# Decode attention over a long cache: heads loaded in pairs with 64 KB rows into three shared buffers, in a hand-scheduled program with a hardware loop

## The chip, the cores and the metric

The kernel runs on one core of a Trainium2 chip. The metric is the device time of one execution in microseconds (us). A "span" is the length of the profiled execution; a run's time is 1.7 to 2.0 us longer than its span (except in run 11). Engines: PE multiplies matrices (PEld is its weight load), DVE does elementwise work and reductions, ACT evaluates functions, SP issues the loads, and 16 DMA engines move the data.

## The reference, cut to what matters

```python
q = (x @ wq).reshape(B, Sq, H, Dh)             # B = Sq = 1, H = 32, Dh = 128
scores = einsum('bhqd,bhkd->bhqk', q, k_cache) * Dh ** -0.5     # Sk = 16384
p = softmax(scores)
a = einsum('bhqk,bhkd->bhqd', p, v_cache).reshape(...) @ wo     # 512 outputs
b = gated MLP of x                             # 512 -> 1792 -> 512, "gMLP" below
out = g * a + (1 - g) * b                      # g: one sigmoid gate
```

K and V are bf16, 4 MiB per head each: 256 MiB for 32 heads, read once. With one query there are about two operations for each loaded element, so the loads are the work.

## The kernel before

Each head's K is one load of 4 MiB with a contiguous 32 KB row in each of 128 partitions, three K buffers deep; V likewise, two deep. The scores are a multiplication on DVE by the broadcast q, then a sum over d by matmuls with an identity and a DVE reduce. The value product has two forms:

```python
def load_k(h):
    t = kv.tile([P, NJ * Dh], BF16, name="k_t", tag="k", bufs=3)      # 32 KB rows
    nc.sync.dma_start(out=t[:], in_=k_src[h])

def scores_mult(h):
    for ks in halves(h):                                              # DVE, in place
        nc.vector.tensor_tensor(out=ks, in0=ks, in1=qh, op=ALU.mult)

def attend(h):              # narrow: V stationary, p moving (1 column); the last 3 heads
    for j in range(NJ):
        nc.tensor.matmul(o_ps[:, h:h + 1], lhsT=v3[:, j, :], rhs=p_sb[h][:, j:j + 1], ...)

def attend_wide(h):         # wide: p stationary, V moving (512 columns); the other 29
    for t in range(NG):
        nc.tensor.matmul(d_ps[32 * g:32 * g + R, :], lhsT=p_sb[h][:, t * R:(t + 1) * R],
                         rhs=vtile[h][:, t * R * Dh:(t + 1) * R * Dh], ...)
# the wide form is followed, every four heads, by a drain (ACT copies d_ps out)
# and a collect (PE picks from the copy each head's own rows)
...                         # gMLP in the middle, about head 22; wo last:
for a, b in ((0, 16), (16, 24), (24, 30), (30, 32)):
    nc.sync.dma_start(out=wo_t[:, a * D:b * D], in_=wo_src[:, a * D:b * D])
```

The softmax here doesn't subtract the row's maximum and nothing guards it: scores larger than these inputs give would overflow.

## Time and profile before

| | before |
|---|---|
| time, median of 12 runs | 661.48 us (661.35 to 662.01) |
| DMA engines busy | 98.8% of the span, for 279.58 MB |
| PE, DVE busy | 77%, 50% |
| instruction fetches by DMA, 16 KB each | 21 |
| packets of 32 KB | 8,192, median 1216 ns |

The page of the kernel before: busy times (engine, us, share, instructions), then the DMA queues (packets, MB, share of 16 engines' span).

```profile
PE 508.3 (77%) x2661; PEld 216.6 (33%) x2661; DVE 331.4 (50%) x167; ACT 28.2 (4%) x88; POOL 0.7 (0%) x6
...
DMA packets 10583, 279.96 MB, mean 424 GB/s; under 512 B 1213, under 2 KB 1214, under 8 KB 1598
...
q1 hardware_dynamic: 10556, 279.58, 98.8%
q8 instruction: 21, 0.34, 0.2%
```

The windows view of the kernel before. The last three columns are the granted PE clock, the DMA share and GB/s.

```profile
core 0: us, PE busy (x) PEld busy (x) DVE busy (x) ACT busy (x) POOL busy (x), PEclk, DMA share, GB/s
...
200.00:300.00 100.00, 80.00 (x337) 32.62 (x337) 53.41 (x21) 3.38 (x14) 0.00 (x0) 0.91 1.00 431
300.00:400.00 100.00, 78.32 (x329) 31.36 (x329) 51.92 (x22) 2.49 (x11) 0.00 (x0) 0.91 1.00 431
...
630.00:640.00 10.00, 7.65 (x144) 5.07 (x142) 1.29 (x3) 0.40 (x2) 0.00 (x0) 0.84 0.95 399
```

Read the pair "1.00 431" first: every DMA engine is busy all the time, while PE and DVE have a fifth and half of the time free. Nothing that only frees PE or DVE can help in this stretch.

The end of the kernel before, in the chain of waits in order of time (start us, us, what):

```profile
632.06 23.85 DMA wo_t<-in_A_wo_dram
655.90 0.05 issue
655.95 1.03 PE a_ps L363 x32
...
657.53 0.21 DVE resT L370
```

The span ends when the loads end, plus about 4 us: 655.90 to 659.8.

### The profile page before, as it was taken

The numbers are of one execution on the slowest core, as the hardware profiler recorded it, in microseconds if no ns is written. First come the engines' busy times: TensorE is split into PE (matmuls) and PEld (weight loads), VectorE is DVE, ScalarE is ACT, GpSimd is POOL, SyncE is SP. The second block draws the span as 40 slices with busy tenths as digits, with TensorE's granted clock in tenths as the row PEclk, the third lists the DMA queues.
The fourth block names the chain that finished last, engine by engine and source line by source line (L and its number), as shares of the span: only waits on it lengthen the run. The fifth ranks groups of instructions, "written<-read, shape, count | busy, mean of one in ns | idle before, by whom it ended". The sixth has DMA issues, their size and how long they took to land.

```text
span 659.8 us, 5835 instructions
## 1 busy us (share of the span) xinstructions
PE 508.3 (77%) x2661; PEld 216.6 (33%) x2661; DVE 331.4 (50%) x167; ACT 28.2 (4%) x88; POOL 0.7 (0%) x6
## 2 busy tenths in 40 slices
PE   2666987786987777898777987739879788877774
PEld 0222432332333323333222333314325233333353
DVE  2567565554456554445654445624566554455600
ACT  0200000000000000000000000000000210000000
POOL 0000000000000000000000000000000000000000
PEclk9888998899988989979878998878979899988975
DMA  9999999999999999999999999999999999999996
GB/s 381 433 425 440 420 439 429 428 433 426 439 421 435 435 426 433 428 431 430 431 434 428 429 433 427 432 430 433 428 431 430 434 427 432 429 430 433 427 415 246
DMA packets 10583, 279.96 MB, mean 424 GB/s; under 512 B 1213, under 2 KB 1214, under 8 KB 1598
## 3 DMA queue, kind: packets, MB, share of 16 engines
q1 hardware_dynamic: 10556, 279.58, 98.8%
q8 instruction: 21, 0.34, 0.2%
q14 instruction: 4, 0.03, 0.0%
q10 hardware_dynamic: 2, 0.00, 0.0%
HBM read 279.58 MB, written 0.00 MB: 424 GB/s over the span
## 4 chain that ended last, share of the span: by engine, by line
DMA 66%; PE 22%; DVE 10%; SPq 1%; issue 0%; DVEq 0%
DMA k_t<-in_A_k_cache_dram 53%; PE s_ps L248 11%; DVE k_t L242 10%; PE d_ps L277 10%; DMA w_in<-in_B_w_in_dram 5%; DMA v_t<-in_A_v_cache_dram 4%; DMA wo_t<-in_A_wo_dram 4%; SPq L78 1%; PE o_ps L265 1%; PE o_ps L288 0%; PE a_ps L363 0%; SPq L339 0%; DVE s_sb L255 0%; SPq L62 0%; PE rT_ps L368 0%
## 5 line engine op out<-in xcount | busy, mean ns | idle before, releaser
L248 PE MATMUL s_ps<-k_t,ident 128*128 128x512 bf16 x1024 | 270.3, 428 | 124.6 <-DVE k_t L242 124.6
L242 DVE TENSOR_TENSOR k_t<-k_t,qb 128x8192 bf16<-128x8192 bf16 x64 | 280.3, 4422 | 165.2 <-DMA k_t<-in_A_k_cache_dram 165.2
L277 PE MATMUL d_ps<-v_t,p_t 128*4 128x512 bf16 x928 | 205.0, 379 | 0.0
L248 PEld LDWEIGHTS <-ident 128*128 128x128 bf16 x1024 | 110.2, 108 | 280.8 <-issue 182.1
L277 PEld LDWEIGHTS <-p_t 128*4 128x4 bf16 x928 | 76.4, 85 | 126.2 <-issue 12.3
L255 DVE TENSOR_REDUCE s_sb<-s_ps 128x64 f32<-128x512 f32 x64 | 44.2, 690 | 126.1 <-PE s_ps L248 126.1
L258 ACT ACTIVATE p_t<-s_sb 128x128 bf16<-128x128 f32 x32 | 9.9, 310 | 396.2 <-DVE s_sb L255 396.2
L106 PE MATMUL q_ps<-wq_t,xb 128*128 128x512 bf16 x32 | 9.2, 458 | 10.5 <-DMA wq_t<-in_A_wq_dram 10.5
L265 PE MATMUL o_ps<-p_t,v_t 128*128 128x1 bf16 x384 | 10.7, 164 | 5.7 <-DMA v_t<-in_A_v_cache_dram 5.7
L265 PEld LDWEIGHTS <-v_t 128*128 128x128 bf16 x384 | 10.3, 100 | 6.1 <-DMA v_t<-in_A_v_cache_dram 6.1
L283 ACT COPY d_sb<-d_ps 128x512 f32<-128x512 f32 x8 | 4.7, 586 | 169.8 <-PE d_ps L277 169.8
L106 PEld LDWEIGHTS <-xb 128*128 128x128 bf16 x32 | 3.6, 113 | 15.8 <-issue 12.4
L288 PEld LDWEIGHTS o_ps<-pick,d_sb 128*128 128x128 f32 x64 | 8.4, 192 | 1.1
L288 PE MATMUL o_ps<-pick,d_sb 128*128 128x4 f32 (+1 forms) x64 | 7.6, 242 | 0.0
L363 PE MATMUL a_ps<-o,wo_t 128*128 128x1 bf16 x128 | 3.9, 166 | 4.3 <-DMA wo_t<-in_A_wo_dram 4.3
L109 DVE CAST qb<-q_ps 128x512 bf16<-128x512 f32 x1 | 0.7, 691 | 11.3 <-PE q_ps L106 11.3
L258 ACT ACTIVATION_READ_ACCUMULATOR p_t<-s_sb 128x1 f32 x32 | 6.0, 188 | 0.0
L350 DVE TENSOR_TENSOR o_sb<-o_ps,rl 128x32 bf16<-128x32 f32 x1 | 0.2, 192 | 11.5 <-PE o_ps L265 11.5
L363 PEld LDWEIGHTS <-wo_t 128*128 128x128 bf16 x128 | 3.7, 104 | 4.5 <-DMA wo_t<-in_A_wo_dram 4.5
L111 ACT CAST qb<-q_ps 128x512 bf16<-128x512 f32 x7 | 4.1, 586 | 16.3 <-PE q_ps L106 16.3
L366 DVE CAST res<-a_ps 128x4 bf16<-128x4 f32 x1 | 0.2, 163 | 8.0 <-PE a_ps L363 8.0
L179 PE MATMUL z_ps<-xb,w_in 128*128 128x1 bf16 x56 | 3.1, 192 | 0.0
(65 smaller groups left out, 25.1 us busy)
## 6 DMA issues: line engine op xcount, KB each, us to landing
k_t<-in_A_k_cache_dram SPq DMA_DIRECT2D x32, 4096.0 KB, 36.7
v_t<-in_A_v_cache_dram SPq DMA_DIRECT2D x31, 4096.0 KB, 27.9
wq_t<-in_A_wq_dram SPq DMA_DIRECT2D x1, 4096.0 KB, 12.4
v_t<-in_A_v_cache_dram SPq DMA_DIRECT2D x1, 2048.0 KB
v_t<-in_A_v_cache_dram SPq DMA_DIRECT2D x2, 1024.0 KB, 16.8
wo_t<-in_A_wo_dram SPq DMA_DIRECT2D x1, 2048.0 KB, 20.4
w_in<-in_B_w_in_dram SPq DMA_DIRECT2D x1, 1792.0 KB, 33.1
wo_t<-in_A_wo_dram SPq DMA_DIRECT2D x1, 1024.0 KB, 22.4
```

The costliest lines, as they stand in the source:

```text
L78: nc.sync.dma_start(out=t[:, a * Dh:b * Dh], in_=v_src[h][:, a * Dh:b * Dh])
L106: nc.tensor.matmul(q_ps[:, :], lhsT=xb[:, c, :], rhs=wq[:, c, nb * QB:(nb + 1) * QB], start=(c == 0), stop=(c == DC - 1))
L111: nc.scalar.copy(out=qb[:, nb * QB:(nb + 1) * QB], in_=q_ps[:, :])
L242: nc.vector.tensor_tensor(out=ks, in0=ks, in1=qh, op=ALU.mult)
L248: nc.tensor.matmul(s_ps[:, :, :], lhsT=ident[:, :], rhs=ks[:, :, i * W:(i + 1) * W], start=(i == 0), stop=(i == NS - 1))
L255: nc.vector.tensor_reduce(out=s_sb[:, s * NH:(s + 1) * NH], in_=s_part[h, s][:, :, :], axis=AX.X, op=ALU.add)
L258: nc.scalar.activation(out=p_t[:], in_=s_sb[:], func=ACT.Exp, scale=inv_sqrt_dh, accum_out=L_sb[:, h:h + 1])
L265: nc.tensor.matmul(o_ps[:, h:h + 1], lhsT=v3[:, j, :], rhs=p_sb[h][:, j:j + 1], start=(j == 0), stop=(j == NJ - 1))
L277: nc.tensor.matmul(d_ps[32 * g:32 * g + R, :], lhsT=p_sb[h][:, t * R:(t + 1) * R], rhs=vtile[h][:, t * R * Dh:(t + 1) * R * Dh], start=(t ...
L283: nc.scalar.copy(out=d_sb[:], in_=d_banks[(h0 // G) % 2][:, :])
L288: nc.tensor.matmul(o_ps[:, h0:h0 + n], lhsT=diag[h0][:, r * Dh:(r + 1) * Dh], rhs=pick[:, r, 0:n], start=(r == 0), stop=(r == R - 1))
L363: nc.tensor.matmul(a_ps[:, c:c + 1], lhsT=wo4[:, k, c, :], rhs=o2[:, k:k + 1], start=False, stop=(k == H - 1), skip_group_check=True)
```

## The change: its intent and its core

The program is rewritten without the tile framework: engines wait on semaphores placed by hand. Two heads go together, so that a load is 8 MiB with 64 KB rows (64 partitions a head). K and V share three buffers in turn: V(i) is loaded into the buffer of K(i) once its scores are summed (the first and the last pair differ). The gMLP moves to the front, PE's stream for most pairs is a hardware loop, and the last two pairs use the narrow form.

```diff
-    k_src = A_k_cache.rearrange("b h (p j) d -> (b h) p (j d)", p=P)
+    k_src = A_k_cache.rearrange("b (i two) (p j) d -> (b i) (two p) (j d)", two=2, p=64)
+    buf = [sb(f"buf{b}", [P, ROW], BF16) for b in range(3)]          # ROW: 64 KB
+    def k_buf(i): return buf[(2 * i) % 3 if i else 1]
+    def v_buf(i): return buf[(2 * i) % 3 if i < NP - 1 else 2]
...
+        if i < NP - 1:
+            load_v(i, w_free if i == 0 else (sum_s, NQ * (i + 1)))   # after the scores of K(i)
+            if i + 2 < NP:
+                load_k(i + 2, (sum_s, NQ) if i == 0 else (pv_s, i))  # after the values of V(i-1)
...
+        full = NIT - 1 if NARROW else NIT
+            with e.Fori(0, full):          # on PE: three pairs a turn
+                iteration(False)
+        if NARROW:
+            iteration(True)                # the last turn written out: pair 14 narrow
...
+    def narrow(e, i, t0, t1):
+        def part(first, last):
+            for t in range(16):
+                for c in range(4):
+                    ins = e.matmul(d_ps[:, 2 * (i - 14):2 + 2 * (i - 14)],
+                                   lhsT=v[:, (4 * t + c) * Dh:(4 * t + c + 1) * Dh],
+                                   rhs=p_t[i % SLOTS][:, 8 * t + c:8 * t + c + 5:4],
+                                   start=(t == 0 and c == 0), stop=(t == 15 and c == 3))
+        if t1 - t0 > 16:
+            with e.Fori(0, (t1 - t0) // 16):
+                part(0, 0)
+        else:
+            ins = part(0, 0)
...
+WO_CUTS = (0, 16, 26, 31, 32)              # before: 0, 16, 24, 30, 32
```

One thing in this diff is not about time. The body of `narrow` does not use its loop's index. Each turn reads the same first 64 of a pair's 256 value rows per partition and starts its sum anew, so for pairs 14 and 15 three quarters of V are loaded and never used.

## The prediction

> **What bounds it now.** The loads. The page gives the 16 DMA engines 9 tenths in 39 of 40 slices, and queue 1 has 98.8% of the engines' span, moving 279.58 MB. The windows view reads 430 to 431 GB/s in every 100 us stretch from 100 to 600 us with a DMA share of 1.00, while PE is busy for 80% and DVE for 52%. No compute engine is near its limit. The "DMA k_t 53%" of the chain of waits is queueing behind other loads, not a wait that can be removed.
>
> **What a packet costs.** The trace's DMA records, sorted by size (medians): 8 KB 313 ns, 16 KB 614 ns, 32 KB 1216 ns. Each doubling adds 27.2 bytes/ns, so a packet costs its bytes at 27.2 GB/s plus about 12 ns. Sixteen engines at 27.2 are 435 GB/s, the ceiling that the Trainium skill states (DMA: Bandwidth & Descriptors, "Where 436 GB/s comes from"); the trace agrees. At that ceiling the unchanged 279.58 MB take 642 us. Before the data comes a 1.5 us start, and after the last wo piece (655.9) 3.9 us; the run is 1.7 us longer than the span. About 649.5 us is therefore a floor for any version that loads the same bytes.
>
> **What the change does.** Bytes, multiplies, 512-wide matmuls and reduces stay the same in total: 64 multiplies of 4.42 us and 1,024 + about 900 wide matmuls. Heads go in pairs: a load is 8 MiB with 64 KB rows, half as many packets and completions. K and V share three buffers in turn. The gMLP moves to the front. The hardware loop shortens the instruction stream. Scheduling is by hand.
>
> - 64 KB packets (if the hardware does not split them): 256 fewer per engine x 12 ns = -2.9 us. All of it counts, because every engine is busy.
> - The dip at 630 to 640 us (399 GB/s, share 0.95) gone: -0.5 us.
> - Fewer instruction fetches (0.34 MB now): -0.5 us at most.
> - The last wo piece needs 4 matmuls rather than 32 (1.03 us): -0.5 us.
> - Narrow attention, one collect for six heads, drains: PE and ACT time, worth nothing.
>
> **New waits, costed.** V0 needs buf0, so it waits for the gMLP, whose small inputs land behind K0, at about 39 us. With some 10 us of small operations it is issued at about 49, and K1 keeps the queue fed to about 57. DVE starts K0 only then; its scores end at about 71, K2 must be issued by 76. K1's scores end at about 94, V1 is needed at about 95: tight, 0 to 2 us lost. From then on V(i) is issued some 8 to 17 us before the queue would run dry. The loop's backward branch may stall PE for a few us (Runtime: NRT & Kernel Launch, "Instruction fetch mechanics": a taken branch outside the prefetched pages waits for a fetch); no trace here shows its size, and that slack covers it.
>
> **Prediction.** 657.5 us, 80% range 653.5 to 661.5. Faster by over 2%: 0.01; within 2%: 0.95; slower by over 2%: 0.04.
>
> **What would show it.** DMA share 1.00 and 431 to 434 GB/s from 100 to 600 us; about half as many large packets, near 2.42 us each; shares below 1 only near 57, 76 and 95 us; PE and DVE busy times within 5% of before; a tail of about 3.4 us after the last landing.
>
> **What would make it wrong.** 64 KB rows split into 32 KB packets: about 660. A buffer freed late in each pair, or a long branch stall: holes in the DMA row once per pair or per loop turn, over 670. Below 650 only if bytes were dropped.

## The result, and the profile after

| | before | after |
|---|---|---|
| time, median | 661.48 us | 657.02 us (656.81 to 657.86, 8 runs) |
| ratio after/before | | 0.9934 (95%: 0.9924 to 0.9944) |
| PE, DVE busy | 508, 331 us | 491, 329 us |
| large packets | 8,192 of 32 KB, 1216 ns | 3,968 of 64 KB, 2420 ns (medians) |
| instruction fetches of 16 KB | 21 | 10 |

The profiled run of the changed kernel took 658.16 us, 1.1 us above the median of its runs: read the last microsecond of its trace with that in mind.

The page of the changed kernel, the same lines as before:

```profile
PE 491.4 (75%) x2733; PEld 212.4 (32%) x2733; DVE 329.0 (50%) x168; ACT 27.0 (4%) x84; POOL 2.2 (0%) x10
...
DMA packets 5818, 279.76 MB, mean 426 GB/s; under 512 B 685, under 2 KB 814, under 8 KB 1070
...
q1 hardware_dynamic: 5804, 279.58, 98.7%
q8 instruction: 10, 0.16, 0.1%
```

The windows view of the changed kernel:

```profile
200.00:300.00 100.00, 79.13 (x344) 31.86 (x342) 46.94 (x19) 3.79 (x14) 0.00 (x0) 0.93 1.01 436
300.00:400.00 100.00, 80.78 (x342) 32.26 (x341) 53.80 (x23) 3.04 (x12) 0.00 (x0) 0.93 1.00 433
...
630.00:640.00 10.00, 8.82 (x320) 8.71 (x317) 0.79 (x3) 0.79 (x5) 0.00 (x0) 0.58 0.94 398
```

The bytes and the bound are the same. The rate in these windows rises from 431 to 433 and 436 GB/s. (A window can read 1.01 because a packet's time and bytes are counted where it starts; use several windows.) The low last window, 398 GB/s at a share of 0.94, is still there.

The end of the changed kernel in the chain of waits:

```profile
629.72 22.52 DMA buf<-in_A_wo_dram
652.24 0.05 issue
652.29 0.98 PE a_ps L505 x24
...
653.82 0.21 DVE res_t L523
```

The wait for the last wo pieces ends 3.66 us earlier than before (652.24 against 655.90). From there to the end of the span it is 4.1 us, against 3.9 before: the tail did not get shorter.

Another reading uses the trace's DMA packet records. Joined end to end, each to the one that starts where it ends, they form 16 sequences of about 17.5 MB, one per DMA engine. Measured from the start of the first large packet:

| | before | after |
|---|---|---|
| mean end of the 16 sequences | 651.4 us | 647.6 us |
| end of the slowest | 654.4 us | 650.4 us |
| idle of the load queue near 95 us | none | 2.8, 1.0 and 0.3 us on three engines (the 1.0 is mostly an instruction fetch) |

An instruction fetch shows in a sequence as a gap of about 1.06 us: that engine carries the fetch instead of a load. The columns come from the two profiled runs, of which that of the changed kernel was 1.1 us slow.

### The profile page after: what moved, and what is told of

Its sections match the earlier page's. It is cut to its first block, busy times and chain, and to the rows that moved or that the text cites. A ratio compares the mean times of both kernels' runs of the same rounds, so it can differ in the third digit from the quotient of the medians.

```text
span 656.3 us, 5975 instructions
## 1 busy us (share of the span) xinstructions
PE 491.4 (75%) x2733; PEld 212.4 (32%) x2733; DVE 329.0 (50%) x168; ACT 27.0 (4%) x84; POOL 2.2 (0%) x10
## 3 DMA queue, kind: packets, MB, share of 16 engines
q1 hardware_dynamic: 5804, 279.58, 98.7%
## 5 line engine op out<-in xcount | busy, mean ns | idle before, releaser
L397 DVE TENSOR_TENSOR buf<-buf,qb 128x8192 bf16<-128x8192 bf16 x64 | 281.5, 4418 | 183.9 <-DMA buf<-in_A_k_cache_dram 183.9
L315 PE MATMUL s_ps<-buf,ident 128*128 128x512 bf16 x1024 | 261.4, 417 | 119.3 <-PEq L313 119.3
L323 PE MATMUL d_ps<-buf,p_t 128*8 128x512 bf16 x896 | 195.7, 379 | 0.0
L315 PEld LDWEIGHTS s_ps<-buf,ident 128*128 128x128 bf16 x1024 | 104.6, 105 | 274.1 <-issue 183.3
L323 PEld LDWEIGHTS d_ps<-buf,p_t 128*8 128x8 bf16 x896 | 76.8, 87 | 117.8 <-issue 5.9
L409 ACT ACTIVATE p_t<-s_sb 64x256 bf16<-64x256 f32 x32 | 13.3, 415 | 499.9 <-DVE s_sb L401 499.8
L335 PE MATMUL d_ps<-p_t,buf 128*128 128x2 bf16 x512 | 13.8, 165 | 1.2 <-DMA buf<-in_A_v_cache_dram 1.2
L335 PEld LDWEIGHTS d_ps<-p_t,buf 128*128 128x128 bf16 x512 | 13.8, 103 | 1.3 <-issue 1.3
L229 PE MATMUL m_ps<-buf,xb 128*64 128x512 bf16 x32 | 5.7, 532 | 10.3 <-DMA buf<-in_A_wq_dram 10.3
L409 ACT ACTIVATION_READ_ACCUMULATOR p_t<-s_sb 64x1 f32 x32 | 5.9, 185 | 0.0
```

The lines of the kernel that those rows point to most:

```text
L229: q_ok = pe.op(lambda e, q_ps=q_ps, s=s, c=c, rhs=rhs: e.matmul(q_ps[64 * s:64 * s + 64, :], lhsT=xb[:, c * P:c * P + 64], rhs=rhs, start= ...
L315: ins = e.matmul(s_ps[c % 2][:, :].rearrange("p (j w) -> p j w", w=W), lhsT=ident[:, :], rhs=k3[:, c * QK:(c + 1) * QK, i * W:(i + 1) * W] ...
L323: ins = e.matmul(d_ps[32 * slot:32 * slot + 8, :], lhsT=p_t[slot][:, 8 * t:8 * t + 8], rhs=v[:, t * 512:(t + 1) * 512], start=(t == 0), st ...
L335: ins = e.matmul(d_ps[:, 2 * (i - 14):2 + 2 * (i - 14)], lhsT=v[:, (4 * t + c) * Dh:(4 * t + c + 1) * Dh], rhs=p_t[i % SLOTS][:, 8 * t + c ...
L397: dve.op(lambda e: e.tensor_tensor(out=k3, in0=k3, in1=q3, op=ALU.mult), wait=wait, inc=(mul_s, 1))
L409: act.op(lambda e, s=s, rows=rows: e.activation(out=p_t[i % SLOTS][rows, :].rearrange("p (t c) -> p t c", c=8)[:, :, 4 * s:4 * s + 4], in_ ...
```

## The experiments

Theory A: the gain is the fixed cost of a packet. Theory B, its rival: the gain comes from scheduling, the shorter instruction stream and the tail. Theory C: instruction fetches cost the load queue. Theory F: the late V1 starves the engines and costs time. Medians of before stayed between 661.30 and 661.48 us in all rounds, so medians of different rounds may be compared to a few tenths.

### 1. 32 KB rows in the changed kernel

```diff
-HALVES = False
+HALVES = True     # every K/V load but the last V as two loads of 32 KiB rows
```

> The changed kernel, but each 8 MiB load of K and V (all but the last V) is two loads whose rows are 32 KiB. Buffers, order of work, matmuls and instruction stream stay. Theory A (the gain is the fixed cost of a packet: 32 KiB packets took 1220 ns on the mean before, 64 KiB packets 2424 ns after, so 16 ns per halved packet, 248 per engine): slower than the changed kernel by 3.5 to 4.5 us, so 660.5 to 661.5 us, nearly all of the way back to before; 32 KiB packets near 1216 to 1220 ns in the DMA records. Theory B (the gain is the hand scheduling, the shorter instruction stream and the tail; packet size is neutral): 657 us, within 1 us of the changed kernel.

Measured: 659.82 us (659.53 to 659.98), ratio to before 0.9976. The page of this run:

```profile
DMA packets 10283, 279.77 MB, mean 425 GB/s; under 512 B 1181, under 2 KB 1310, under 8 KB 1566
...
q8 instruction: 10, 0.16, 0.1%
```

With the packets doubled and the fetches as in the changed kernel, it is 2.8 us slower. So packet size is 2.8 of the 4.5 us. That is the 2.9 us of the prediction, made from medians, rather than the 3.5 to 4.5 us I then expected from mean durations. (The number of loads doubles too: 31 more packets of 4 bytes per engine, 9 ns each, at most 0.3 us of the 2.8.) Theory B, as the whole story, is refuted; about 1.6 us of the gain are left for what it names.

### 2. 16 KB rows

```diff
-    LD = 32 if HALVES else 16
-    whole = (0, ROW // 2, ROW) if HALVES else (0, ROW)
+    LD = 64
+    whole = (0, ROW // 4, ROW // 2, 3 * ROW // 4, ROW)
```

> As the run with halves, but each load is four loads with 16 KiB rows. 16 KiB packets took 614 ns (median) in both traces, so four cost 2456 ns against 2421 for one of 64 KiB: +35 ns x 248 per engine. Theory A: +8.5 to +12 us against the changed kernel, so 665.5 to 669 us, about three times the loss of the halves. Theory B: within 1 us of 657.

Measured: 664.05 us (664.01 to 664.38), 7.0 us above the changed kernel and slower than before. The first halving cost 2.8 us for 248 more packets per engine (11 ns each), the second 4.2 us for 496 more (8.5 ns each). A fixed cost of about 10 ns per packet explains both, a little less than the 12 ns of the prediction and below the range I expected. The records agree when read by spacing: on one engine the next packet starts 3 to 4 ns before the last one ends, and the medians from start to start between 100 and 600 us, 612, 1214 and 2418 ns for 16, 32 and 64 KB (runs 2, 1 and the changed kernel), give 10 ns a packet.

### 3. The hardware loop written out

```diff
-UNROLL = False
+UNROLL = True     # the hardware loop written out
```

> The changed kernel with the hardware loop on PE written out, so more instructions are fetched by DMA and no backward branch is taken. Theory C (instruction fetches cost the load queue: each 16 KiB fetch was about 1.06 us on its engine; 10 after, 21 before): about 10 to 12 more fetches in the trace, 0.5 to 1.0 us slower, 657.5 to 658.2 us. Theory D (the branch costs more than fetches do): faster by 0.3 us or more. Theory E (neither matters, they hide in slack): within 0.3 us of the changed kernel.

Measured: 658.46 us (658.33 to 659.5), 1.4 us above the changed kernel. The queue of instruction fetches in this run:

```profile
q8 instruction: 19, 0.31, 0.2%
```

Nine more fetches of about 1.06 us each are 9.5 us of one DMA engine, 0.6 us on the mean of 16, and the load packets took another 0.5 us per engine. The medians differ by more than this sum of 1.1 us, and by more than I expected. Between the two profiled runs (659.15 and 658.16 us) it is only 1.0 us, as is the difference in the end of the slowest engine (651.4 against 650.4). Some engines here carried two or three fetches, where in the changed kernel none carried more than one; that this uneven load makes up the rest is argued, not shown. So the loop is worth about 1.4 us, of which 0.6 is the fetches' own time. The rival D, a costly backward branch, would have the other sign on the whole.

Together, 2.8 for the packets and 1.4 for the loop make 4.2 of 4.5 us, if the two add up, which no single run shows. The rest, 0.3 us, is not assigned.

### 4. Small inputs first

```diff
-SMALL_FIRST = False
+SMALL_FIRST = True     # four small loads ahead of K0, so the gMLP runs 20 us earlier
```

> The changed kernel with its four small inputs loaded ahead of K0 rather than behind it, so the gMLP runs at about 20 us, V0 is issued some 20 us earlier and K0's multiplies start when K0 lands (about 38 us) rather than after the gMLP (about 45 us). Theory F (the late V1 issue at 94.06 us starves some DMA engines: the trace's packets show three engines idle for 2.8, 1.0 and 0.3 us at about 95 us, and the slowest engine sets the end): no idle engine there, V1 issued near 87 us, 0.5 to 2 us faster, 655 to 656.5 us. Rival (that idle time fell on engines that were ahead and is absorbed): within 0.3 us of 657.0.

Measured: 656.98 us (656.82 to 657.14). V1 was issued at 88.23 us rather than 94.06, and the idle time near 95 us was gone. The time was the same. Theory F falls, its rival stands: the idle engines were ahead of the others at that moment.

### 5. More work on DVE

```diff
+        dve.op(lambda e: e.tensor_reduce(out=junk[:, c * QK:(c + 1) * QK], in_=s_ps[c % 2]...),
+            wait=[(sum_s, NQ * i + c + 1)])      # every reduce twice, small inputs first
```

> The changed kernel with small inputs first, and every reduce of the scores done twice, the first time into a tile nobody reads: 64 x 0.69 = 44 us more work on DVE (329 us busy becomes 373). If compute is off the path, as both the prediction and this explanation say, the time stays within 0.5 us of 657.0 (V1 is then issued near 94 us, as late as in the changed kernel). If DVE or PE sets the pace anywhere in the steady state, 5 us or more are lost (2.8 us in each of 16 pairs would be 44).

Measured: 656.90 us (656.77 to 657.09). The groups of DVE in this run (line, engine, operation, out<-in, shapes, count | busy us, mean ns | idle before):

```profile
L402 DVE TENSOR_REDUCE junk<-s_ps 128x64 f32<-128x512 f32 x64 | 44.1, 689 | 65.7 <-PE s_ps L316 65.7
L406 DVE TENSOR_REDUCE s_sb<-s_ps 128x64 f32<-128x512 f32 x64 | 43.6, 681 | 0.0
```

44 us of useless work cost nothing. DVE is off the critical path at this size of load.

### 6. Wide values for the last two pairs

```diff
-NARROW = True
+NARROW = False    # pairs 14 and 15 in the wide form, with drain and collect
```

> The changed kernel with the last two pairs in the wide form too (p as the stationary operand, then drain and collect), the cut of the last V unchanged at 192 of 256. The prediction held the narrow form worth nothing. Against that: the last 64 rows land about 8 us before the end, then come 16 wide matmuls at 379 ns each (3.5 us warm, 6.8 us at the halved clock of this stage), a drain of 0.6, a collect of 1.0, 1.2 us of transposes, and 128 wo matmuls of 3.4 us. So 1.5 to 4 us slower, 658.5 to 661 us, if that chain ends after the last wo piece; if the prediction's 'worth nothing' holds, within 0.3 us of 657.0, or slightly faster because the last turn joins the loop and 2 to 4 fetches fall away.

Measured: 668.78 us (667.74 to 669.01), 11.8 us above the changed kernel: three times the most that I expected, and slower than before. PE in time order in this run:

```profile
622.95 3.61 PE L315 MATMUL s_ps<-buf,ident 128*128 128x512 bf16 x16 [1.32 <-PEq L313]
626.50 13.98 PE L323 MATMUL d_ps<-buf,p_t 128*8 128x512 bf16 x64
...
642.44 13.98 PE L323 MATMUL d_ps<-buf,p_t 128*8 128x512 bf16 x64
```

In the chain of waits of this run no load stands in the last 10 us, and the wo matmuls come far behind the loads:

```profile
659.37 0.20 DVE o L500
659.57 0.14 issue
659.70 4.52 PE a_ps L505 x128
```

I had counted only the 16 matmuls behind the last piece of V. But after the scores of the last K both remaining pairs are still to be done, 14 us each, and that runs past the landing of wo, here before 652 us. A low clock is not the reason: the granted clock was 1.00 from 627 to 654 us here, not halved as I had assumed. In the steady state the loads hide PE's time; at the end it is worth its full length. The changed kernel needs 6.84 and 6.97 us for the two pairs, so its end is covered by the loads.

### 7. Wide values, last V cut later

```diff
-V_CUT = 192
+V_CUT = 240       # with NARROW = False and the small inputs first
```

> As the wide form, with the last V cut at 240 of 256, so only 4 wide matmuls follow its last piece, and the small inputs first. All V rows are read, and all five turns are in the hardware loop. If a fetch costs 0.1 to 0.15 us of the whole (from the unrolled run: 9 more fetches, +1.4 us), 3 fewer give 656.5 us, the fastest version; the tail after the last wo landing is as long as in the changed kernel. If the wide form's tail still binds, 657.5 us or more.

Measured: 668.53 us (668.15 to 668.56), as slow as run 6, against an expected 656.5. It confirms the reading of run 6: the 28 us of wide work count, not the last few matmuls. It had only 6 fetches.

### 8. The narrow form mended

```diff
-        def part(first, last):
-            for t in range(16):
...
+        for t in range(t0, t1):            # all 64 groups, written out, no loop
+            for c in range(4):
+                ins = e.matmul(d_ps[:, 2 * (i - 14):2 + 2 * (i - 14)],
+                               lhsT=v[:, (4 * t + c) * Dh:(4 * t + c + 1) * Dh],
+                               rhs=p_t[i % SLOTS][:, 8 * t + c:8 * t + c + 5:4],
+                               start=(t == 0 and c == 0), stop=(t == NG - 1 and c == 3))
```

> The changed kernel with its narrow attention mended. As written, each turn of that loop reads the same first 64 of a pair's 256 value rows per partition, so the last two pairs' outputs leave out three quarters of V; here the loop is written out over all of them. Same number of matmuls (512), same bytes loaded, some 770 more PE instructions in the stream, so about 3 more 16 KiB fetches (13 rather than 10). Theory C (a fetch costs the load queue): +0.2 to 0.6 us against 657.0. Rival (reading the right rows costs something itself, or the mended text waits more): +1 us or more. Also: whether the comparison with the reference tells the two apart at all (it said correct of the changed kernel).

Measured: 660.37 us (659.62 to 662.28), 3.4 us above the changed kernel, with the same 512 matmuls and 12 fetches; theory C allowed at most 0.6, its rival 1 or more. The tail in the chain of waits of the profiled run (the slowest of the five, 662.28 us):

```profile
627.63 1.43 PE d_ps L334 x57
629.06 1.86 issue
630.92 3.55 PE d_ps L334 x128
634.47 2.65 issue
637.12 2.04 PE d_ps L334 x71
...
641.07 2.00 issue
643.07 3.57 PE d_ps L334 x128
646.64 2.62 issue
649.26 2.12 PE d_ps L334 x73
...
652.90 4.52 PE a_ps L496 x128
```

PE runs 128 matmuls in 3.55 us and pauses for 1.9 to 2.7 us, four times, 9.1 us in all. "issue" means that it waited for nothing that the profile shows. Compare the changed kernel's PE in time order, where a loop of 64 matmuls gives the same count with no pause:

```profile
629.49 6.84 PE L335 MATMUL d_ps<-p_t,buf 128*128 128x2 bf16 x256
...
637.99 6.97 PE L335 MATMUL d_ps<-p_t,buf 128*128 128x2 bf16 x256 [1.18 <-DMA buf<-in_A_v_cache_dram]
```

The comparison with the reference said "correct" of both. It cannot tell them apart: computed on a CPU from the reference's inputs, the whole attention part of the output is at most 5.8e-5, the gMLP part up to 0.061, and leaving out three quarters of V for four heads moves an output by at most 2.2e-5. A wrong attention passes here.

### 9. The wrong rows, written out

Run 8 changed two things, the rows that are read and the form of the code. This one changes the form alone.

```diff
-                               lhsT=v[:, (4 * t + c) * Dh:(4 * t + c + 1) * Dh],
+                               lhsT=v[:, (4 * (t % 16) + c) * Dh:(4 * (t % 16) + c + 1) * Dh],
...                             # against run 8; p_t, start and stop likewise
```

> The run that mended the narrow attention came out at 660.37 us, 3.4 us above the changed kernel; its trace shows PE pausing four times for 1.9 to 2.7 us in the tail with 'issue' as the reason, about every 128 matmuls. Here the same loop is written out, but reads the wrong first 64 rows again, as the changed kernel does (a wrong result on purpose, of a size that the comparison did not see). Theory G (the pauses are PE waiting for its instruction stream: 128 pairs of weight load and matmul are 16 KiB of instructions and run in 3.5 us; a loop body of 64 pairs is fetched once): the same four pauses, 660.4 us within 0.5. Rival (the pauses come from reading the right rows): no pauses, about 657 us.

Measured: 659.91 us (659.01 to 662.9), and three pauses of 1.85 to 2.62 us, one fewer than expected:

```profile
634.38 2.03 PE L334 MATMUL d_ps<-p_t,buf 128*128 128x2 bf16 x71 [2.10 <-issue]
...
641.16 3.57 PE L334 MATMUL d_ps<-p_t,buf 128*128 128x2 bf16 x128 [1.85 <-issue]
647.36 2.10 PE L334 MATMUL d_ps<-p_t,buf 128*128 128x2 bf16 x73 [2.62 <-issue]
```

The rows that are read don't matter; writing the code out does. The plain remedy, a loop whose body uses its index, was not run. The pauses come about every 128 matmuls, which with their weight loads are 256 instructions. The Trainium skill (Runtime: NRT & Kernel Launch, "Instruction fetch mechanics") says that instructions are refilled in blocks of 16 KiB, 256 instructions; the period agrees. The views do not name the wait, but the DMA packet records give the times of the 16 KB fetches. In run 8 one ends at 629.50, 635.83, 641.64 and 647.82 us, and PE goes on 1.3 to 1.4 us after each. The same holds for all twelve such pauses in the tails of runs 8 to 12: each ends 1.3 to 1.6 us after the end of a fetch. So the pauses are, by all that the records show, waits for instructions.

### 10. A version that reads all of V: pair 14 wide in the loop, pair 15 narrow

```diff
+        full = NIT                          # all five turns in the hardware loop
...
-            iteration(True)
...
+    HT = 2                                  # only pair 15 comes from the narrow form
...
+K15_CUT = True                              # last K in four loads; and small inputs first
```

> A version that reads all of V: pair 14 in the wide form within the hardware loop (64 wide matmuls, few instructions), pair 15 narrow and written out, the last K in four loads so that its scores end some 14 us earlier, small inputs first. If the tail of PE is what costs the mended version its 3.4 us, the scores of K15 end near 612 rather than 627 us, wide V14 runs from its landing near 625 to 639, narrow V15 ends at 647 to 649 and o2 is ready at 648 to 650: the wo pieces then bind again, 657 to 658 us. If only the packets and fetches matter, it is 657.2. If instruction pauses hit V15's 256 matmuls fully (two of 2.3 us), 659 us.

Measured: 659.25 us (657.7 to 659.43; two of the five took under 658). Its loads ended the earliest so far: the slowest DMA engine at 648.3 us after the first packet, against 649.2 in the run with the small inputs first and 650.4 in the changed kernel. Seven fetches go with that, against ten. But PE came too late: pauses of 1.75 and 0.80 us, and the wo matmuls ended at 654.43 us.

### 11. The same with V14 in two loads

```diff
+                    attend(e, v_buf(s), s, 0, NG // 2)       # pair 14
+                    e.wait_ge(ld_h, 16)
+                    attend(e, v_buf(s), s, NG // 2, NG)
```

> As the hybrid, with V14 in two loads waited for one by one, so half of its wide matmuls run before its second half lands: PE is then done with V14 near 632 us and waits for V15's last pieces, as in the changed kernel. All rows read. Expected 656.8 to 657.5 us: as fast as the changed kernel, 3 us faster than the mended one. If it is not faster than the hybrid with V14 whole, PE's tail was already hidden there.

Measured: 659.02 us (658.11 to 659.47), above the range expected. The last turn is written out again here (10 fetches). In the profiled run, the fastest of the five at 658.11 us, PE was done in time and the last wo pieces bound. The other four took 0.8 to 1.4 us more, but not within the program: their spans are 655.8 to 656.0 us, no longer than the 656.0 of the profiled run. What differs is the time outside the span, 3.0 to 3.5 us against 2.1 in the profiled run and at most 2.0 in all other runs. Its cause is open. Within its span this version is as fast as that of run 12 (655.6 to 656.0).

### 12. The two parts together

```diff
...                                         # against run 10
-                attend(e, v_buf(s), s, 0, NG)
+                if s == 2:                  # every third V in two loads, inside the loop
+                    attend(e, v_buf(s), s, 0, NG // 2)
+                    e.wait_ge(ld_h, 16).then_inc(ld_h, -16)
+                    attend(e, v_buf(s), s, NG // 2, NG)
```

> The version meant to beat both kernels while reading all of V: as the hybrid (pair 14 wide inside the loop, pair 15 narrow and written out, last K in four loads, small inputs first), with every third V in two loads so that half of V14's wide matmuls run before its second half lands; the loop keeps the instruction stream short (7 fetches in the hybrid). The hybrid's loads ended 1 us earlier than those of any other version, but PE's tail held it: its 128 wo matmuls ended at 654.4 us, 1.4 us after they could have. If both parts add up (loads as early, PE hidden), 656 to 657 us, at or just below the changed kernel; if the extra packets (about 60 per engine, 12 ns each) and pauses of PE's instruction stream eat it, 657.5 to 659.5 us, like the other two hybrids.

Measured: 657.64 us (657.36 to 657.74), ratio to before 0.9943. PE's end in time order:

```profile
617.47 13.98 PE L324 MATMUL d_ps<-buf,p_t 128*8 128x512 bf16 x64
...
635.84 3.79 PE L335 MATMUL d_ps<-p_t,buf 128*128 128x2 bf16 x136 [2.35 <-DMA buf<-in_A_v_cache_dram]
642.19 3.36 PE L335 MATMUL d_ps<-p_t,buf 128*128 128x2 bf16 x120 [2.56 <-issue]
...
648.34 3.56 PE L496 MATMUL a_ps<-o,buf 128*128 128x1 bf16 x126 [1.07 <-issue]
```

This is the fastest version here whose code, as read, computes the reference in full (the comparison cannot confirm it): 3.7 us under before. It is 0.6 us over the changed kernel, which skips part of V. It does not beat both. Its loads end at 648.3 us, 2 us before those of the changed kernel's profiled run; the two pauses of PE (2.56 and 1.07 us) now hold the end.

## Why the prediction was right or wrong, point by point

The time was right: 657.5 us forecast, 657.02 measured, within 2% as said. The parts were not all right, and that the total came out to 0.5 us is partly luck: the loop was worth 0.9 us more than allowed for, while the 1.0 us credited to the dip and the tail does not show in the records.

- **"The loads bound it"**: right. DMA at 98.7% after, the rate at 431 to 436 GB/s, and 44 us of extra DVE work cost nothing (run 5). The skill's ceiling of 435 GB/s (DMA: Bandwidth & Descriptors, "Where 436 GB/s comes from") agrees with the records' 27.2 GB/s per engine beyond the fixed part of a packet.
- **"64 KB packets, -2.9 us"**: right in mechanism and size. The hardware kept 64 KB rows as one packet (2420 ns, forecast 2.42 us), and halving them costs 2.8 us (run 1).
- **"Fewer instruction fetches, -0.5 us at most"**: the term was mis-sized. Writing the loop out costs 1.4 us (run 3). I averaged the fetches over 16 engines, which accounts for 0.6 us of it; the rest is not fully explained.
- **"The dip at 630 to 640 us gone, -0.5 us"**: wrong. It reads 398 GB/s at 0.94 after, and the joined packet records of before show no engine idle there apart from fetches. A 10 us window was read as idle time.
- **"The last wo piece needs 4 matmuls rather than 32, -0.5 us"**: wrong. The 32 of before were two pieces that landed together, 24 and 8. After, 24 matmuls follow (20 and 4), 0.98 us against 1.03, and the tail is 4.1 us against 3.9.
- **"Narrow attention ... worth nothing"**: wrong. Without it the kernel takes 668.78 us (run 6). The forecast of the total did not suffer, because the changed kernel has the narrow form and I counted nothing for it.
- **"V0 at 49, K2 at 71, V1 at 94, 0 to 2 us lost"**: the times were right (46.56, 69.63, 94.06). Of the three places named, the joined records show idle time near 95 us alone: on three engines, one of them mostly for an instruction fetch, and no time was lost (run 4).
- **"The loop's backward branch may stall PE, the slack covers it"**: no cost of it was seen; the loop is a gain.
- **Not forecast at all**: the changed kernel is short in instructions at its end because of a loop that reads the wrong rows. With all rows read by code written out it is 660.37 us, and three quarters of the gain are gone (run 8), to the form of the code and not to the rows (run 9).

## What to carry to other kernels

While the DMA engines are full, the terms that counted here were bytes, fixed costs per packet and whatever else uses those engines; take a packet's cost from the start-to-start times of two sizes in the DMA records (twice that of 32 KB less that of 64 KB), and expect a gain of a fraction of a per cent. An engine with time to spare in the steady state still needs its work at the end counted by itself: list what is left after the last load but one, in order, with durations and with the instructions that it needs. And ask whether the test can see the part that was changed: here it could not see the attention at all.

## What the Trainium skill lacked or had wrong

- DMA: Bandwidth & Descriptors gives a fixed cost per DMA, a per-packet overhead for small descriptors and about 10.5 ns a packet for a 4 KB transfer issued from GpSimd, but no cost of a large packet issued from SP. The records here show medians of 313, 614, 1216 and 2420 ns for 8, 16, 32 and 64 KB, about 27.2 GB/s plus 12 ns, and about 10 ns a packet in the time of the kernel (runs 1 and 2). A row of 64 KB is one packet in the records.
- Runtime: NRT & Kernel Launch, "Instruction fetch mechanics", says that crossing a block is "mostly hidden" and that the dispatch of instructions is slower than the refill. For PE with small matmuls (128 pairs in 3.55 us) it was not hidden: pauses of 1.9 to 2.7 us, about one for each 256 instructions, each ending 1.3 to 1.6 us after a fetch (runs 8 and 9).
- The same section gives the cost of branches as a reason against loops ("prefer full unrolling where possible"). Here the loop with three pairs a turn was 1.4 us faster than the same code written out (run 3). The fetches ride on the DMA engines that the loads fill; no page has that cost, about 1.06 us of one engine for each 16 KB, 0.6 us of the 1.4.
